# Attention into GEGLU on one core: a new step order in the first two batches, and out-projections rotating over three PSUM banks

## The chip, the cores and the metric

The kernel runs on one core of a Trainium2 chip. The metric is the device time of one execution in microseconds. Times inside an execution come from one profiled run, counted from the start of its span.

## The reference

A causal attention with 16 extra "beacon" keys that every query may see, for 8 batches of 8 heads with 576 tokens of 64 channels, is followed by a GEGLU block on the 4608 tokens of 512 channels.

```python
k_all, v_all = [beacon_k, k], [beacon_v, v]              # 16 + 576 keys
scores = q @ k_all.T / sqrt(64)                          # causal mask on the 576
a = softmax(scores)
x = (a @ v_all) -> (4608, 512)                           # heads side by side
out = (gelu(x @ w_gate) * (x @ w_val)) @ w_out           # d_ff = 1536, float32 out
```

## The kernel before

**Data flow.** Per batch, the heads are taken in four pairs (`m` = 0 to 3). For a pair, `scores` computes the transposed scores in four chunks S0 to S3 (512, 480, 464 and 208 columns for each of the two heads) into one of two PSUM buffers of two banks (tag `s`), and ScalarE takes the exponential of each chunk straight out of it (L205). `mask` zeroes the diagonal blocks, on POOL (`a` steps, L293) or by a table on VectorE (`d` steps, L290). `sums` (Z) multiplies the exponentials by ones into the two `z` banks, and adds the values of the first 64 queries, for which it needs value tile 0 alone. `values` (V) multiplies by all five value tiles into the one `x` bank, in the tile order 0, 2, 4, 1, 3. `invert` (I: transpose, reciprocal, transpose back) and `scale` (M: one product for the z part, one for the x part) run on VectorE and write `xT_sb`. A batch's attention is written by hand as five strings of steps, one for each pair and a last one; each engine executes its own instructions in that order.

**Gate and value.** The tokens are then taken in nine chunks of 512. For each of 12 tiles `gate_val` does 4 + 4 matmuls into an `s` buffer, ScalarE applies gelu (`ge_sb`), VectorE multiplies (`hT_sb`, L386). `gate_val_first` does the first tile's three earlier k-steps, then a filler, and then the step that needs the last pair of heads.

**Out-projection.** `o(n)` issues the next `n` of 48 matmuls per chunk: four groups (`ti`) of 12 (`fi`), each group into `o_ps`, a bank of a pool with one buffer (tag `o`). After a group VectorE copies it out (L424) and SyncE's queue writes it to `out` (L426). `O12` and the like are such calls within attention. At the end, `o(4)` follows each gate tile of the last chunk, and `o(OUT_UNITS)` does the last chunk's own 48.

**Loads.** POOL issues the loads, in order and interleaved with its masks: `r` a pair's q and k of batch 0, `y` a value tile of batch 0 (y0 also its beacon), `w` a third of the gate and value weights, `N3` three of the queued loads for the next batch. In batches 0 and 1, q and k are transposed on TensorE (`q1x`: pair 1's q through bank x; also o and z) and copied to `qkT` by VectorE (L246). `h3x` is three idle matmuls into bank x, `heat(n)` the same into bank o.

**What sets the order.** The step strings, the order of calls and the rotating PSUM and SBUF buffers: an instruction whose buffer is still being read waits, and with it all that is behind it on its engine.

Of the kernel before, what the change touches and what calls it, by code (L numbers as in the profile page):

```python
# [7 lines left out]
P = 128  # L8
B, H, S, NB, D = 8, 8, 576, 16, 64
SK = S + NB  # L10
N_TOK = B * S
D_MODEL = 512
D_FF = 1536
F_TILES = D_FF // P
K_CHUNKS = D_MODEL // P
CH = 512
N_CHUNKS = N_TOK // CH
NPAIR = H // 2
OUT_UNITS = (CH // P) * F_TILES
# [26 lines left out]
Z0 = 448  # L46
# [3 lines left out]
FP32 = mybir.dt.float32  # L50
# [8 lines left out]
def kernel(  # L59
# [12 lines left out]
    nc = tc.nc  # L72
    keep = tc.keep_in_program_order
# [7 lines left out]
    opool = ctx.enter_context(tc.tile_pool(name="opool", bufs=4))  # L81
    psum_s = ctx.enter_context(tc.tile_pool(name="psum_s", bufs=2, space=bass.MemoryType.PSUM))
    psum_x = ctx.enter_context(tc.tile_pool(name="psum_x", bufs=1, space=bass.MemoryType.PSUM))
    psum_o = ctx.enter_context(tc.tile_pool(name="psum_o", bufs=1, space=bass.MemoryType.PSUM))
# [11 lines left out]
    wo_sb = const.tile([P, F_TILES, D_MODEL], BF16, name="wo_sb", tag="wo_sb")  # L96
# [26 lines left out]
    def load_runs(b, m):  # L123
        for out_ap, in_ap in runs(b, m):
            dma(out_ap, in_ap)
# [75 lines left out]
    def mm(out_ap, lhsT, rhs, start, stop, **kw):  # L201
        keep(nc.tensor.matmul(out_ap, lhsT, rhs, start=start, stop=stop, **kw))  # L202
# [4 lines left out]
    def bank(tag, dtype, n, name):  # L207

        pool = psum_o if tag == "o" else psum_x
        if tag == "z":  # L210
            n *= 2
        return pool.tile([P, n], dtype, name=name, tag=tag)
# [108 lines left out]
    def sums(b, m):  # L321
        z_ps = z_of[b * NPAIR + m] = psum_x.tile([P, 1024], FP32, name="z_ps", tag="z")
        attend(b, m, z_ps, Z0, True, 0, SPLIT)
        attend(b, m, z_ps, Z0 + SPLIT, True, SPLIT, S)
        attend(b, m, z_ps, 0, False, 0, SPLIT, start=False)

    def values(b, m):
        x_ps = x_of[b * NPAIR + m] = psum_x.tile([P, S - SPLIT], FP32, name="x_ps", tag="x")
        attend(b, m, x_ps, 0, False, SPLIT, S)
# [32 lines left out]
    h_of, gv_of = {}, {}  # L362

    def gate_val_mms(ci, fi, kks):
        if fi == 0 and ci not in h_of:
            h_of[ci] = hpool.tile([P, F_TILES, CH], BF16, name="hT_sb", tag="hT_sb")
        if (ci, fi) not in gv_of:
            gv_of[ci, fi] = psum_s.tile([P, 2, CH], FP32, name="gv_ps", tag="s")
        gv_ps = gv_of[ci, fi]
        for w in range(2):  # L370
            for kk in kks:
                mm(
                    gv_ps[:, w, :],
                    (wg_sb, wv_sb)[w][:, kk, fi * P : (fi + 1) * P],
                    xT_sb[:, kk, ci * CH : (ci + 1) * CH],
                    kk == 0,
                    kk == K_CHUNKS - 1,
                    skip_group_check=True,
                )

    def gate_val_end(ci, fi):
        gv_ps = gv_of.pop((ci, fi))
        ge_sb = fpool.tile([P, CH], BF16, name="ge_sb", tag="ge_sb")
        act(ge_sb, gv_ps[:, 0, :], ACT.Gelu)
        keep(
            nc.vector.tensor_tensor(  # L386
                out=h_of[ci][:, fi, :], in0=gv_ps[:, 1, :], in1=ge_sb, op=ALU.mult
            )
        )

    def gate_val(ci, f0, f1):
        for fi in range(f0, f1):
            gate_val_mms(ci, fi, range(K_CHUNKS))
            gate_val_end(ci, fi)

    def gate_val_first(ci, fill, n, tiles=1):

        for fi in range(tiles):
            gate_val_mms(ci, fi, range(K_CHUNKS - 1))
        fill(n)  # L400
        for fi in range(tiles):
            gate_val_mms(ci, fi, [K_CHUNKS - 1])
            gate_val_end(ci, fi)

    out_done = [0]
    o_ps_of = [None]

    def o(n):
        for _ in range(n):
            ci, u = divmod(out_done[0], OUT_UNITS)  # L410
            ti, fi = divmod(u, F_TILES)
            if fi == 0:
                o_ps_of[0] = psum_o.tile([P, D_MODEL], FP32, name="o_ps", tag="o")
            o_ps = o_ps_of[0]
            mm(
                o_ps,
                h_of[ci][:, fi, ti * P : (ti + 1) * P],
                wo_sb[:, fi, :],
                fi == 0,
                fi == F_TILES - 1,  # L420
            )
            if fi == F_TILES - 1:
                o_sb = opool.tile([P, D_MODEL], FP32, name="o_sb", tag="o_sb")
                keep(nc.vector.tensor_copy(o_sb, o_ps))  # L424
                n0 = ci * CH + ti * P
                keep(nc.sync.dma_start(out=out[n0 : n0 + P, :], in_=o_sb))  # L426
            out_done[0] += 1

    def exp_table():
        keep(nc.scalar.preload_act_table_set(SET_EXP))  # L430
# [4 lines left out]
    def attention(b, *slots, extra=None):  # L435


        for m, slot in enumerate(slots):
            for step in slot.split():
                kind, n = step[0], step[1:]  # L440
                if kind == "S":
                    scores(b, m, *(int(c) for c in n))
                elif kind == "Z":
                    sums(b, int(n or m - 1))
                    if not n:
                        invert(b, m - 1)
                elif kind == "I":
                    invert(b, int(n))
                elif kind == "V":
                    values(b, int(n or m - 1))  # L450
                    if not n:
                        scale(b, m - 1)
                elif kind == "M":
                    scale(b, int(n))
                elif kind == "O":
                    o(int(n))
                elif kind in "adkq":
                    extra[kind](b, *n)
                else:
                    extra[kind](*n) if kind in "kqrwLhyad" else extra[kind](n)  # L460
# [9 lines left out]
            out=ident,  # L470
            in_=ident,
# [10 lines left out]
            out=tri,  # L482
            in_=tri,
# [4 lines left out]
            channel_multiplier=-1,  # L488
        )
    )  # L490
    for w, copies, n in ((0, [(S, dve_copy)], 0), (1, [(114, act_copy), (S, act_copy)], 1)):
        t0 = psum_s.tile([P, 2048], BF16, name="t0_ps", tag="s")
        trans(0, 0, w, t0, copies)
        heat(n)
# [3 lines left out]
    def load_next(n):  # L498
# [4 lines left out]
    extra = {  # L503
        "k": lambda b, m, tag: trans_in(tag, b, int(m), 1),
        "q": lambda b, m, tag: trans_in(tag, b, int(m), 0),
        "a": lambda b, m, c: mask(b, int(m), int(c)),
        "d": lambda b, m, c: mask(b, int(m), int(c), by_table=True),
        "r": lambda m: load_runs(0, int(m)),
        "h": lambda n, tag: heat(int(n), tag),
        "y": lambda t: load_v_tile(0, int(t)),  # L510
        "N": lambda n: load_next(int(n)),
# [3 lines left out]
    for m in range(1, NPAIR):  # L515
        queue.extend(runs(1, m))
    attention(
        0,
        "r2 h3x S0 k1o q1x S1 r3 y2 S2 d00 y0 q2o y1 k2x S3 d02 y3 d01 d03", "S0 y4 S1 w0 Z0 d10 S2 I0 a11 S3 k3x", "a12 S0 q3o S1 S2 a13 V0 M0 Z1 V1 w1 S3", "a21 I1 a20 a23 M1 S0 S1 a22 w2 Z2 V2 I2 S2 S3", "h3o a30 a31 a32 M2 a33 Z3 V3 I3 M3",
        extra=extra,  # L520
    )
    load_next(99)
    gelu_table()
    gate_val_first(0, heat, 2, 1)
    gate_val(0, 1, 7)
    trans_in("z", 1, 0, 1)
    gate_val(0, 7, 7 + 1)
    trans_in("x", 1, 0, 0)
    gate_val(0, 7 + 1, F_TILES)
    load_v(1)  # L530
    load_out_w()

    for b in range(1, B):
        exp_table()
        if b + 1 < B:
            queue.extend(qk_loads(b + 1))
        if b == 1:
            attention(b, "S0 S1 k1x a01 q1z S2 k3o d00 S3 d03 d02", "S0 N3 k2o S1 a11 a10 Z0 q2o I0 S2 a12 V0 M0 S3 a13", "S0 S1 q3o a21 Z1 I1 a20 S2 V1 a22 S3 M1", "S0 a23 S1 a30 a31 Z2 S2 I2 V2 a32 M2 S3 a33 O12", "Z3 N3 V3 I3 M3 N3 O12", extra=extra)
        elif b == 2:
            attention(b, "S0 O12 N3 S1 S2 O12 S3 N3", "S0 Z0 I0 S1 S2 O12 S3 V0 N3", "S0 S1 M0 Z1 V1 I1 S2 S3 O7", "S0 S1 M1 Z2 V2 I2 S2 S3 N2 M2", "O2 O3 Z3 I3 V3 M3 O12", extra=extra)  # L540
        else:
            attention(b, "O5 S0 S1 O7 S2 S3 O2 N3", "S0 S1 Z0 I0 V0 S2 M0 S3 O10 N3", "S0 S1 Z1 V1 I1 S2 S3 M1 O12 N3", "S0 S1 Z2 V2 I2 M2 S2 S3 O5 N2", "Z3 I3 V3 M3", extra=extra)
        gelu_table()
        if b + 1 < B:
            load_next(99)
            load_v(b + 1)
        gate_val_first(b, o, 0 if b == 1 else 0 if b == 2 else 7)
        if b + 1 < B:
            xbar_transpose(b + 1)
        gate_val(b, 1, F_TILES)  # L550
    o((N_CHUNKS - 2) * OUT_UNITS - out_done[0])
    for fi in range(F_TILES):
        gate_val(N_CHUNKS - 1, fi, fi + 1)
        o(4)
    o(OUT_UNITS)


# [28 lines left out]
```

## Time and profile before

| what | value |
|---|---|
| time, median of 3 runs | 408.98 us (407.93 to 410.36) |
| the profiled execution's own time | 410.23 us |
| its span, first to last instruction | 408.5 us |
| TensorE busy | 389.9 us, 95% of the span |
| ScalarE, VectorE, POOL busy | 189.2, 197.8, 163.9 us |
| mean granted TensorE clock | 0.982 |
| first gate and value matmul of batch 0, of batch 1 | 29.18 us, 76.53 us |
| start of the last four out-projection groups | 391.47, 395.01, 398.54, 402.07 us |

A row of the profile's groups gives the line, the engine and operation, the tiles written and read, the count, the busy time and the mean duration of one. Matmuls are pipelined: the 512-column ones take 379 ns each but follow each other every 216 ns, so that distances between starts say more than durations. A window's row gives the busy time of each engine (TensorE, its weight loads, VectorE, ScalarE, POOL, each with its number of instructions), then the granted TensorE clock, the DMA share and GB/s. A wait's row gives who waited for what: us in total, times, the longest.

### The profile page before, as it was taken

How to read it: one execution, taken by the hardware profiler on the slowest of the kernel's cores; microseconds unless marked ns; L12 is line 12 of the kernel's file. 1: busy time of each engine (PE TensorE's matmuls, PEld its weight loads, DVE VectorE, ACT ScalarE, POOL GpSimd, SP SyncE). 2: the span in 40 equal slices, each digit the busy share in tenths (PEclk: the TensorE clock that was granted, in tenths of full speed). 3: DMA queues.
4: the chain of work that ended last, by engine and by line, in shares of the span. 5: the costliest groups of instructions: out<-in, count | busy, mean ns of one | idle time of the engine just before them, and what ended most of it. 6: DMA issues, size and time to landing. Idle time of an engine off the chain costs nothing.

```text
span 408.5 us, 6704 instructions
## 1 busy us (share of the span) xinstructions
PE 389.9 (95%) x2665; PEld 179.2 (44%) x2665; DVE 197.8 (48%) x341; ACT 189.2 (46%) x255; POOL 163.9 (40%) x296
## 2 busy tenths in 40 slices
PE   7789979999999999999999999999999999999975
PEld 3444444444444444444444444444444444444432
DVE  2674458543473446543654266435733564333321
ACT  3743368135653387238633764366534853312200
POOL 8767134901871069404960297019900420000000
PEclk9799979999999999999999999999999999999999
DMA  7999950990989249962997099909991100001012
GB/s 98 180 181 173 153 62 4 155 160 9 147 77 162 38 48 133 111 109 37 128 123 114 27 100 129 137 8 112 105 148 36 54 27 26 0 27 51 26 53 77
DMA packets 139279, 36.19 MB, mean 89 GB/s; under 512 B 126960, under 2 KB 134640, under 8 KB 139248
## 3 DMA queue, kind: packets, MB, share of 16 engines
q0 software_dynamic: 104112, 19.15, 59.4%
q1 hardware_dynamic: 35136, 16.62, 18.3%
q8 instruction: 21, 0.34, 0.4%
q14 instruction: 10, 0.08, 0.1%
HBM read 38.27 MB, written 9.44 MB: 117 GB/s over the span
## 4 chain that ended last, share of the span: by engine, by line
PE 89%; DVE 4%; ACT 2%; POOL 2%; DMA 1%; issue 1%; POOLq 0%; DVEq 0%
PE gv_ps L202 46%; PE o_ps L202 24%; PE s_ps L202 7%; PE z_ps L202 6%; PE x_ps L202 5%; DVE o_sb L424 2%; DMA v_sb<-in_v_dram 1%; ACT expT L205 1%; DVE zt L337 1%; DVE rec L342 1%; PE t_ps L223 1%; POOL q L114 1%; POOL k L114 1%; DVE xT_sb L354 0%; POOL v_sb L114 0%
## 5 line engine op out<-in xcount | busy, mean ns | idle before, releaser
L205 ACT ACTIVATE ge_sb<-gv_ps 128x512 bf16<-128x512 f32 x108 | 64.5, 598 | 158.9 <-PE gv_ps L202 158.9
L386 DVE TENSOR_TENSOR hT_sb<-gv_ps,ge_sb 128x512 bf16<-128x512 f32 x108 | 74.7, 692 | 118.0 <-ACT ge_sb L205 118.0
L293 POOL TENSOR_SCALAR_AFFINE_SELECT expT<-expT 128x256 bf16<-128x256 bf16 (+2 forms) x151 | 55.4, 395 | 163.8 <-ACT expT L205 149.6
L205 ACT ACTIVATE expT<-s_ps 128x1024 bf16<-128x1024 f32 (+3 forms) x128 | 103.3, 862 | 36.4 <-PE s_ps L202 33.7
L202 PE MATMUL gv_ps<-xT_sb,wg_sb 128*128 128x512 bf16 x432 | 112.2, 379 | 0.3 <-DVE xT_sb L354 0.3
L202 PE MATMUL gv_ps<-xT_sb,wv_sb 128*128 128x512 bf16 x432 | 112.2, 379 | 0.0
L202 PE MATMUL o_ps<-wo_sb,hT_sb 128*128 128x512 bf16 x432 | 103.3, 380 | 4.0 <-DVE o_sb L424 3.8
L202 PEld LDWEIGHTS <-wv_sb 128*128 128x128 bf16 x432 | 42.3, 98 | 51.5 <-issue 0.6
L202 PEld LDWEIGHTS <-wg_sb 128*128 128x128 bf16 x432 | 41.6, 98 | 50.8 <-issue 1.6
L202 PEld LDWEIGHTS <-hT_sb 128*128 128x128 bf16 x432 | 40.0, 98 | 52.3 <-issue 6.9
L424 DVE COPY o_sb<-o_ps 128x512 f32<-128x512 f32 x36 | 24.9, 690 | 44.5 <-PE o_ps L202 44.5
L202 PE MATMUL s_ps<-qkT 64*128 64x80 bf16 (+5 forms) x384 | 41.9, 292 | 4.7 <-ACT expT L205 3.2
L337 DVE STREAM_TRANSPOSE zt<-z_ps 128x576 f32<-128x576 f32 x32 | 25.1, 783 | 28.6 <-PE z_ps L202 28.6
L114 POOL DMA_DIRECT2D v_sb<-in_v_dram x40 | 34.0, 889 | 0.0
L202 PE MATMUL z_ps<-expT,ones 80*64 80x80 bf16 (+5 forms) x384 | 30.5, 295 | 1.0 <-DVE xT_sb L354 0.9
L202 PEld LDWEIGHTS <-qkT 64*128 64x128 bf16 x384 | 14.8, 95 | 36.5 <-issue 32.9
L202 PE MATMUL x_ps<-expT,v_sb 128*64 128x512 bf16 (+4 forms) x320 | 28.8, 311 | 0.0
L114 POOL DMA_DIRECT2D k_sb<-in_k_dram x30 | 25.7, 855 | 0.8 <-DMA out_dram<-o_sb 0.3
L114 POOL DMA_DIRECT2D q_sb<-in_q_dram x30 | 25.8, 860 | 0.2
L342 DVE STREAM_TRANSPOSE rec<-rz 128x576 f32<-128x576 f32 x32 | 24.9, 778 | 1.1
L354 DVE TENSOR_TENSOR xT_sb<-x_ps,rec 128x512 bf16<-128x512 f32 x32 | 21.8, 681 | 1.8 <-PE x_ps L202 1.8
L202 PEld LDWEIGHTS <-ones 128*64 128x64 bf16 (+1 forms) x384 | 15.8, 113 | 13.5 <-issue 7.7
(36 smaller groups left out, 125.0 us busy)
## 6 DMA issues: line engine op xcount, KB each, us to landing
out_dram<-o_sb SPq DMA_DIRECT2D x36, 256.0 KB, 2.3
v_sb<-in_v_dram POOLq DMA_DIRECT2D x24, 128.0 KB, 5.2
q_sb<-in_q_dram POOLq DMA_DIRECT2D x24, 128.0 KB, 4.4
k_sb<-in_k_dram POOLq DMA_DIRECT2D x18, 128.0 KB, 4.8
wg_sb<-in_moe_w_gate_dram POOLq DMA_DIRECT2D x3, 512.0 KB, 7.0
wv_sb<-in_moe_w_val_dram POOLq DMA_DIRECT2D x3, 512.0 KB, 8.6
wo_sb<-in_moe_w_out_dram POOLq DMA_DIRECT2D x1, 1536.0 KB, 14.0
q<-in_q_dram POOLq DMA_DIRECT2D x8, 144.0 KB, 5.4
```

The lines of the kernel that those rows point to most:

```text
L114: keep(nc.gpsimd.dma_start(out=out_ap, in_=in_ap))
L202: keep(nc.tensor.matmul(out_ap, lhsT, rhs, start=start, stop=stop, **kw))
L205: keep(nc.scalar.activation(out_ap, in_ap, func, **kw))
L223: keep(nc.tensor.transpose(out_ap, in_ap, ident[0:n, 0:n]))
L293: nc.gpsimd.affine_select(out=d, in_=d, pattern=[[0, 2], [1, DIAG[t]]], compare_op=ALU.is_ge, fill=0.0, base=base, channel_multiplier=-1,)
L337: keep(nc.vector.transpose(zt, z_of[i][:, Z0 : Z0 + S]))
L342: nc.vector.transpose(rec.rearrange("p (n j) -> p n j", j=32), rz.unsqueeze(2).to_broadcast([P, NBLK, 32]))
L354: nc.vector.tensor_tensor(out=xT_sb[:, m, b * S + q0 : b * S + q1], in0=acc[:, 0 : q1 - q0], in1=rec[:, q0:q1], op=ALU.mult,)
L386: nc.vector.tensor_tensor(out=h_of[ci][:, fi, :], in0=gv_ps[:, 1, :], in1=ge_sb, op=ALU.mult)
L424: keep(nc.vector.tensor_copy(o_sb, o_ps))
```

## The change

In batch 0's strings, value tile y0 is loaded ahead of pair 3's q and k, y4 and y1 to y3 follow in another order, pair 0's S1 and S2 come ahead of two transposes, S3 behind those of pair 2, and the sums of pair 0 come after pair 1's S1. One heating matmul is added ahead of k's first transposes and one behind them; three in the last string and two in the first gate tile are left out. Batch 1's strings are reordered in the same manner (a transposition of q earlier, three loads earlier, one heating matmul), batch 2's slightly. The transpositions for batch 1 stand two and three gate tiles later.

The out-projections outside of attention, from the last chunk but one on, take their bank by `tags[ti % 3]` from o, x and z. Three in place of four out-projection matmuls follow each gate tile of the last chunk. The very last group is done by `o_last` in two halves of 256 columns, in banks o and x, each with a copy and a write of its own (the first from ScalarE's queue).

```diff
-    def o(n):
+    def o(n, tags="o"):
...
             if fi == 0:
-                o_ps_of[0] = psum_o.tile([P, D_MODEL], FP32, name="o_ps", tag="o")
-            o_ps = o_ps_of[0]
+                o_ps_of[0] = bank(tags[ti % len(tags)], FP32, D_MODEL, "o_ps")
+            o_ps = o_ps_of[0][:, 0:D_MODEL]
...
+    def o_last():
+
+        ci, ti = N_CHUNKS - 1, CH // P - 1
+        n0 = ci * CH + ti * P
+        half = D_MODEL // 2
+        for x, tag in enumerate("ox"):
+            cols = slice(x * half, (x + 1) * half)
+            o_ps = bank(tag, FP32, CH, "o_ps")[:, 0:half]
+            for fi in range(F_TILES):
+                mm(o_ps, h_of[ci][:, fi, ti * P : (ti + 1) * P], wo_sb[:, fi, cols], fi == 0, fi == F_TILES - 1)
+            o_sb = opool.tile([P, half], FP32, name="o_half", tag="o_half")
+            keep(nc.vector.tensor_copy(o_sb, o_ps))
+            keep((nc.scalar, nc.sync)[x].dma_start(out=out[n0 : n0 + P, cols], in_=o_sb))
...
-    for w, copies, n in ((0, [(S, dve_copy)], 0), (1, [(114, act_copy), (S, act_copy)], 1)):
+    for w, copies, n in ((0, [(S, dve_copy)], 1), (1, [(114, act_copy), (S, act_copy)], 2)):
...
-        "r2 h3x S0 k1o q1x S1 r3 y2 S2 d00 y0 q2o y1 k2x S3 d02 y3 d01 d03", "S0 y4 S1 w0 Z0 d10 S2 I0 a11 S3 k3x", "a12 S0 q3o S1 S2 a13 V0 M0 Z1 V1 w1 S3", "a21 I1 a20 a23 M1 S0 S1 a22 w2 Z2 V2 I2 S2 S3", "h3o a30 a31 a32 M2 a33 Z3 V3 I3 M3",
+        "h3z r2 S0 S1 k1o q1z S2 k2x q2o y0 r3 y4 y1 S3 d01 a00 y2 a02", "S0 a03 S1 Z0 y3 d10 I0 w0 S2 k3x a11 S3", "S0 a13 a12 q3o S1 S2 V0 M0 w1 Z1 V1 I1 M1 S3 a20", "S0 S1 a21 a22 a23 Z2 V2 I2 M2 w2 S2 S3 a31", "a30 a32 a33 Z3 I3 V3 M3",
...
-    gate_val_first(0, heat, 2, 1)
-    gate_val(0, 1, 7)
+    gate_val_first(0, heat, 0, 1)
+    gate_val(0, 1, 10)
     trans_in("z", 1, 0, 1)
-    gate_val(0, 7, 7 + 1)
+    gate_val(0, 10, 10 + 1)
     trans_in("x", 1, 0, 0)
-    gate_val(0, 7 + 1, F_TILES)
+    gate_val(0, 10 + 1, F_TILES)
...
-            attention(b, "S0 S1 k1x a01 q1z S2 k3o d00 S3 d03 d02", "S0 N3 k2o S1 a11 a10 Z0 q2o I0 S2 a12 V0 M0 S3 a13", "S0 S1 q3o a21 Z1 I1 a20 S2 V1 a22 S3 M1", "S0 a23 S1 a30 a31 Z2 S2 I2 V2 a32 M2 S3 a33 O12", "Z3 N3 V3 I3 M3 N3 O12", extra=extra)
+            attention(b, "S0 N3 k1z S1 a01 q1x k3o d00 S2 a02 S3 q2o d03", "N3 S0 S1 k2o Z0 a11 S2 a10 I0 a12 V0 S3 M0", "S0 a13 q3o S1 a21 Z1 S2 h1o a20 I1 S3 a22 V1", "M1 S0 S1 a23 Z2 I2 a31 a30 V2 M2 S2 a32 S3 a33 O12", "Z3 I3 V3 M3 O12 N3", extra=extra)
         elif b == 2:
-            attention(b, "S0 O12 N3 S1 S2 O12 S3 N3", "S0 Z0 I0 S1 S2 O12 S3 V0 N3", "S0 S1 M0 Z1 V1 I1 S2 S3 O7", "S0 S1 M1 Z2 V2 I2 S2 S3 N2 M2", "O2 O3 Z3 I3 V3 M3 O12", extra=extra)
+            attention(b, "S0 O12 N3 S1 S2 O12 S3 N3", "S0 Z0 S1 S2 I0 O12 S3 N3 V0", "S0 S1 M0 Z1 V1 S2 S3 O6 I1", "S0 M1 S1 Z2 V2 I2 S2 M2 S3", "O2 O4 Z3 V3 I3 N2 M3 O12", extra=extra)
...
-    o((N_CHUNKS - 2) * OUT_UNITS - out_done[0])
+    o((N_CHUNKS - 2) * OUT_UNITS - out_done[0], "oxz")
     for fi in range(F_TILES):
         gate_val(N_CHUNKS - 1, fi, fi + 1)
-        o(4)
-    o(OUT_UNITS)
+        o(3, "oxz")
+    o(OUT_UNITS, "oxz")
+    o_last()
```

## The prediction

> **What bounds the kernel now.** I read the engine table first, then the clock row, the chain of waits, the waits table, and the timeline and windows of the two stretches where TensorE is idle.
>
> ```profile
> PE 389.9 (95%) x2665; PEld 179.2 (44%) x2665; DVE 197.8 (48%) x341; ACT 189.2 (46%) x255; POOL 163.9 (40%) x296
> PEclk9799979999999999999999999999999999999999
> PE 89%; DVE 4%; ACT 2%; POOL 2%; DMA 1%; issue 1%; POOLq 0%; DVEq 0%
> ```
>
> TensorE is the bound: 389.9 of 408.5 us, and 89% of the chain. Only two things can be won: its 18.6 us of idle time, and time in which it is busy at a low clock (the two 7s in the clock row). By the windows view the idle time is 7.0 us before 35, 2.8 us between 50 and 70, 7.2 us after 380, and 1.6 us elsewhere.
>
> ```profile
> PE o_ps L202 <- DVE o_sb L424: 3.8, 5, 1.1
> PE s_ps L202 <- ACT expT L205: 3.2, 11, 0.5
> PE z_ps L202 <- DMA v_sb<-in_v_dram: 1.6, 1, 1.6
> ```
>
> ```profile
> 391.47 2.75 PE L202 MATMUL o_ps<-wo_sb,hT_sb 128*128 128x512 bf16 x12 [1.15 <-DVE o_sb L424]
> 394.26 0.69 DVE L424 COPY o_sb<-o_ps 128x512 f32<-128x512 f32 x1 [2.84 <-PE o_ps L202]
> 395.01 2.75 PE L202 MATMUL o_ps<-wo_sb,hT_sb 128*128 128x512 bf16 x12 [0.78 <-DVE o_sb L424]
> 404.86 0.69 DVE L424 COPY o_sb<-o_ps 128x512 f32<-128x512 f32 x1 [2.84 <-PE o_ps L202]
> ```
>
> The tail: each out-projection group of 12 matmuls waits until VectorE has copied the one bank out, four times running.
>
> ```profile
> 11.62:15.03 3.41, 1.55 (x22) 0.81 (x18) 1.82 (x7) 2.29 (x3) 3.08 (x6) 1.00 2.30 154
> 15.03:18.45 3.42, 3.19 (x39) 1.82 (x40) 2.78 (x6) 2.21 (x3) 1.49 (x3) 0.51 1.42 200
> 18.45:21.86 3.41, 3.41 (x28) 1.83 (x26) 1.35 (x3) 1.97 (x3) 1.78 (x5) 0.50 1.24 206
> 52.58:55.99 3.41, 2.03 (x48) 1.50 (x48) 2.19 (x5) 3.38 (x5) 0.00 (x0) 1.00 0.17 27
> 55.99:59.41 3.42, 2.90 (x31) 1.43 (x32) 2.33 (x7) 2.90 (x4) 2.95 (x5) 0.51 0.19 14
> 59.41:62.82 3.41, 3.41 (x38) 1.81 (x35) 1.99 (x4) 1.20 (x2) 1.42 (x4) 0.50 1.08 70
> ```
>
> The start: second column TensorE's busy time, third from the end its clock. Twice, a thin stretch (1.55 and 2.03 us busy of 3.41) is followed by 6.8 us at half clock, in batch 0's attention and in batch 1's. The windows before and after with 2.35 us busy or more were not followed by one.
>
> [...]
>
> **Part 1, the tail.** Before, the last gate group issues 389.30 minus its 1.73 us; four o matmuls follow and would end issuing at 390.17. The next group starts at 391.47, so 1.30 us are lost; the other three start 3.53 us apart for 12 x 0.216 = 2.59 us of issue, 0.94 lost each. Sum 1.30 + 3 x 0.94 = 4.1 us. After: the loop puts 3 in place of 4 matmuls behind each gate step, so its end comes 12 x 0.216 = 2.59 us earlier, and 12 matmuls of chunk 7's fourth group are left to cover the last gelu (0.60) and product (0.69). Groups take o, x, z by ti % 3, and ti is 3 then 0 at the chunk's border: both take bank o, so one wait of 0.94 stays. The groups of ti 0, 1, 2 and the halves (o, x) each find a bank freed two groups before. So 4.1 - 0.9 = 3.2 us gained. The last group in halves: [...]nothing, if the weight loads (98 ns) stay hidden; unhidden, [...]+2.4 us[...]. I take +0.05. The copy that ends the chain goes from 512 to 256 columns: the 64- and 512-column products take 0.224 and 0.681, so 1.02 ns a column, and the copy falls from 0.69 to about 0.42: -0.27. The last write moved its 256 KB in about 0.7 of its 2.0 us; half of that is about -0.3; the first half leaves earlier on ScalarE's idle queue. **Tail: -3.7 us** (-1.3 to -4.0).
>
> **Part 2, batch 0.** All q, k, v and weight transfers are issued by POOL in order. Moving y0 (two transfers) ahead of r3 (two), y1 and y2: before, q3, k3, v2, the beacon and v0 landed between 11.1 (k2, read off the k transpose at 11.09) and 15.1, 544 KB in 4.0 us. v0 is now ahead of q3, k3 and v2 (416 KB), so it lands 3.1 us earlier, near 12.0; the wait of 1.58 us goes. Next late: k2. S3 of pair 0 is now behind the transposes of k2 and q2, so it cannot start before 11.09 + 0.49 + 0.38 = 12.0, and ScalarE, which is then done with S0 to S2 (exps 1.02, 0.97, 0.94 from 8.0), idles from 10.9 to 12.2. From there I walk the queues with the rows' durations (S0 to S3 0.3, 0.3, 0.3, 0.2 on TensorE; transposes 0.5 and 0.4; Z and V 0.8 each; exps as above, S3 0.51):
>
> exps of pair 0's S3 at 12.2, pair 1's four 12.8 to 16.2, pair 2's S0 16.2 to 17.2. Z0 at 13.2 (its mask a03 is done by POOL at 13.2). Pair 2's S2 takes the score buffer that S0 leaves at 17.2, V0 runs 17.6 to 18.4, Z1 from 18.4. Before, Z1 began at 20.7 and the first gate's last matmuls at 31.41. The chain between them, Z, invert (0.8 + 0.3 + 0.8 on VectorE), scale's first part 0.23, then Z again, three times, is the same in both orders: 3.2 us a turn, 10 us with everything at full clock (before, Z1 itself ran at half). So the gate's last step comes at 28.4 with no low clock: -3.0 us.
>
> With the low clock: the new order has 1.8 us of work between 8.2 and 11.6 (q1, k1, S2, then nothing until k2 lands at 11.09), thinner than what tripped before. On the same grid the spell runs 11.6 to 18.4. In it q2, S3, S0, S1, Z0, S2, k3 take double: pair 1's S0 is computed 13.3, its S2 (behind Z0, 15.4) 16.0, pair 2's S0 17.7, exp to 18.9, V0 19.3, Z1 20.1, gate 30.1: **-1.3 us**. I take this one.
>
> Costs hidden: y3 waits on POOL behind a03 and is issued at 13.2 to 14.0; with 4.3 to 6.2 us to landing it is there at 17.5 to 19.5, while V0's last two matmuls want it at 18.2 (full clock, up to 1.3 us lost) or 20.0 (low clock, nothing). w0 is issued about 1.5 us later, lands near 23 to 24, wanted at 26: covered by 2 us; w1 and w2 have more. The extra heat ahead of k's transposes fits in the wait for k (5.24 to 5.95); that behind them puts S0 0.1 us later (counted: exps from 8.0, not 7.84). The five removed heats lay ahead of waits (0.51 and 0.33 us on VectorE), the one added in batch 1 costs 0.22 at most (in the 0.7 above). Moving the z transposes from after tile 6 to after tile 9 leaves the q copy 2.2 us after its transposes begin, before ScalarE's exp table is in: nothing.
>
> **Part 3, batch 1.** ScalarE has its table at 54.0 and four pairs of exps, 3.4 us each. With the gate's end kept at 52.0 for comparison, the new order (S1 after one transpose, q2 before pair 1's scores, I1 after S2) walks to the next gate's first matmul at 73.8 at full clock; before it was 76.5. On the same grid, shifted by 1.3 us, the window 53.9 to 57.3 holds 2.0 us of work and trips again; k2, Z0, S2, V0, S3, S0 then run at half speed to 64.1, and the walk ends at 76.6. **0 us**, with -2.7 as the other end and +0.7 above (the spell lies in denser work). The N3 in slot 0 has POOL's idle time before 56 (14 us idle); the N3 that stays ahead of a11 holds POOL to 60.1, and Z1 wants a11's mask at 61.4 or later. Those transfers go to a ring slot that nobody reads yet.
>
> **Part 4, batch 2.** The 60 o matmuls are cut otherwise (7, 2, 3 become 6, 2, 4), I0, V0 and I1 are shifted; TensorE has 0.4 us idle there, of which 0.27 lies in slot 0, untouched. 0, within 0.3 either way (I1 may make Z2 late).
>
> **Sum:** -3.7 - 1.3 + 0 + 0 = -5.0 us. The profiled execution took 410.23 us (span 408.5 and 1.7 around it), the upper end of the runs (407.93 to 410.36); it becomes 405.2, and the median 404.0. Two spells' shifting place would explain such a spread.
>
> **Rivals.**
> A, forecast, 0.64: both spells stay, 404.0, 402.6 to 405.4 with the spread of runs.
> B, 0.22: the extra heats and the denser order lift one or both spells. -3.7 - 3.0 - 2.7 = -9.4 with both, so 399.6; with one about 402. For it: the windows at 2.35 us stayed up, a small margin. Against: both thin stretches come from waits (k2's landing, the table load) that no edit takes away.
> C, 0.11: the tail does less than it says, the half-width weight loads lie bare (+2.4), or one more spell falls in the first gate, whose two heats were removed: 6.8 us at half clock, all on the path, +3.4. 406.4 to 407.4.
> D, 0.03, slower: low clock at the gates. Each spell there costs 3.4 us in full; two more than today give -5.0 + 6.8 = +1.8 (410.8), still no difference, three +5.2 (414.2). It decides from the third. Against it: once a gate runs, it is busy 3.41 of 3.41 us.
> That the banks do not rotate (pools serialising them) would leave -1.9, 407: in C.
>
> A difference of 0.5% (2.0 us) is about what a measurement here can tell. Faster by more, 0.90 (A, B, part of C); within, 0.07; slower, 0.03. Range 400.4 to 406.5: A with its spread, most of B, the near end of C. I put the time at 403.8, A with a little of its lower side.
>
> **What would show it.** Right: o_ps waits on o_sb down from five to two, one of 0.8 us near 390; the last copy about 0.42 us; no z_ps wait for v_sb; the gate's first step near 30; low clock from about 11.6 or a window beside it, and again in batch 1. Wrong: 256-column matmuls over 0.15 us apart, an x_ps wait for v_sb over 1 us, or low clock after 30 in a gate.

## The result, and the profile after

The changed kernel takes 402.46 us (median of 4 runs, 401.96 to 403.17) where the kernel before takes 409.14 (407.93 to 410.36): a ratio of 0.9838, 95% interval 0.9804 to 0.9872. That is 6.7 us or 1.6% less. The forecast was 403.8 in a range of 400.4 to 406.5. The profiled execution took 403.17 us, with a span of 401.5.

The same parts of the page of the changed kernel: engines, clock, chain.

```profile
PE 387.7 (97%) x2675; PEld 179.8 (45%) x2675; DVE 197.1 (49%) x338; ACT 188.9 (47%) x255; POOL 164.9 (41%) x300
PEclk9899969999999999999999999999999999999999
PE 91%; DVE 4%; DMA 1%; POOL 1%; ACT 1%; issue 1%; POOLq 0%
```

TensorE is still the bound. Its busy time fell by 2.2 us although 10 matmuls were added: the stretches at a clock of 0.50 within it are 10.2 us long in all, for 13.7 before. Its idle time fell from 18.6 to 13.8 us.

Four rows of its waits (who waited for what: total, times, longest):

```profile
PE z_ps L202 <- DVE xT_sb L354: 1.3, 1, 1.3
PE o_ps L202 <- DVE o_sb L425: 1.1, 2, 0.8
PE t_ps L223 <- DMA k<-in_k_dram: 0.9, 1, 0.9
PE gv_ps L202 <- DVE xT_sb L354: 0.8, 1, 0.8
```

The wait of z_ps for v_sb is gone, and k2's landing is the wait in its place, as forecast. The o_ps waits went from five to two. The 1.3 and 0.8 us are the z bank and the last pair, late at the end of batch 0 now that TensorE has less to do there.

The timeline of the end:

```profile
387.35 10.55 PE L202 MATMUL o_ps<-wo_sb,hT_sb 128*128 128x512 bf16 x60 [0.78 <-DVE o_sb L425]
396.63 0.42 DVE L441 COPY o_half<-o_ps 128x256 f32<-128x256 f32 x1 [0.62 <-PE o_ps L202]
397.09 0.37 ACTq L442 DMA_DIRECT2D out_dram<-o_half  x1
397.94 0.42 DVE L441 COPY o_half<-o_ps 128x256 f32<-128x256 f32 x1 [0.89 <-PE o_ps L202]
398.39 0.33 SPq L442 DMA_DIRECT2D out_dram<-o_half  x1
```

One wait of 0.78 us, bank o taken twice running; then 60 matmuls without a gap.

The windows around the two thin stretches (second column TensorE's busy time, third from the end its clock):

```profile
8.96:12.37 3.41, 1.97 (x49) 1.28 (x44) 2.51 (x6) 2.76 (x5) 3.41 (x6) 1.00 1.63 172
12.37:15.78 3.41, 3.41 (x37) 1.92 (x37) 2.23 (x7) 2.43 (x3) 3.41 (x7) 0.50 2.05 135
15.78:19.20 3.42, 2.91 (x44) 1.69 (x46) 2.61 (x6) 3.42 (x5) 2.64 (x7) 1.00 1.16 179
49.95:53.36 3.41, 1.96 (x46) 1.33 (x45) 3.10 (x7) 3.38 (x5) 0.00 (x0) 0.99 1.60 170
53.36:56.80 3.44, 3.44 (x45) 2.22 (x46) 1.70 (x5) 3.01 (x4) 3.27 (x6) 0.50 0.46 29
56.80:60.20 3.40, 3.40 (x28) 1.17 (x26) 2.69 (x6) 1.44 (x3) 1.85 (x5) 0.51 1.65 108
```

Again each low spell follows a window of which under 60% was busy (1.97 and 1.96 us of 3.41), and the two starts, 12.37 and 53.36, lie 41.0 us apart, 12 times 3.41, as 15.03 and 55.99 do in the profile before. In batch 0 the spell is one window long here (3.41 us), not two (6.83). Being thin is not enough to tell, though: the window from 22.60 us on, 2.14 us busy, was followed by no spell in this profile (the clock is 1.00 from 15.78 to 53.33).

The two timelines laid side by side, by starts of TensorE's matmuls:

| mark | before | after | gained up to it |
|---|---|---|---|
| last k-step of batch 0's first gate tile | 31.41 | 28.82 | 2.59 |
| first gate matmul of batch 1 | 76.53 | 72.77 | 3.76 |
| out-projection group ahead of the last chunk's gate | 356.50 | 352.74 | 3.76 |
| end of the span | 408.5 | 401.5 | 7.0 |

So the profile puts 2.6 us in batch 0, 1.2 in batch 1, nothing in batches 2 to 7 and 3.2 in the tail. What it can't say is how much of the first two is the order and how much the clock.

### The profile page after: what moved, and what is told of

Its sections match the earlier page's. It is cut to its first block, busy times and chain, and to the rows that moved or that the text cites. A ratio compares the mean times of both kernels' runs of the same rounds, so it can differ in the third digit from the quotient of the medians.

```text
span 401.5 us, 6727 instructions
## 1 busy us (share of the span) xinstructions
PE 387.7 (97%) x2675; PEld 179.8 (45%) x2675; DVE 197.1 (49%) x338; ACT 188.9 (47%) x255; POOL 164.9 (41%) x300
## 4 chain that ended last, share of the span: by engine, by line
PE 91%; DVE 4%; DMA 1%; POOL 1%; ACT 1%; issue 1%; POOLq 0%
PE gv_ps L202 46%; PE o_ps L202 24%; PE z_ps L202 7%; PE s_ps L202 7%; PE x_ps L202 5%; DMA k<-in_k_dram 1%; DVE o_sb L425 1%; PE t_ps L223 1%; ACT expT L205 1%; DVE zt L337 1%; DVE rec L342 1%; POOL q L114 0%; DVE xT_sb L354 0%; DVE qkT L246 0%; DVE rz L339 0%
## 5 line engine op out<-in xcount | busy, mean ns | idle before, releaser
L293 POOL TENSOR_SCALAR_AFFINE_SELECT expT<-expT 128x256 bf16<-128x256 bf16 (+2 forms) x155 | 57.0, 398 | 157.6 <-ACT expT L205 145.1
L202 PE MATMUL o_ps<-wo_sb,hT_sb 128*128 128x512 bf16 (+1 forms) x444 | 102.8, 374 | 1.3 <-DVE o_sb L425 1.1
L202 PEld LDWEIGHTS <-hT_sb 128*128 128x128 bf16 x444 | 41.2, 98 | 48.2 <-issue 3.4
L354 DVE TENSOR_TENSOR xT_sb<-x_ps,rec 128x512 bf16<-128x512 f32 x32 | 21.8, 681 | 1.0 <-PE x_ps L202 1.0
```

Of the source, the lines that this page charges most:

```text
L293: nc.gpsimd.affine_select(out=d, in_=d, pattern=[[0, 2], [1, DIAG[t]]], compare_op=ALU.is_ge, fill=0.0, base=base, channel_multiplier=-1,)
L354: nc.vector.tensor_tensor(out=xT_sb[:, m, b * S + q0 : b * S + q1], in0=acc[:, 0 : q1 - q0], in1=rec[:, q0:q1], op=ALU.mult,)
```

## The experiments

Beside its time every run has its mean granted clock. A spell is a stretch at a clock of 0.50, one or two windows of 3.41 us long in the profiles before and after, so 2 x (1 - clock) x time is the time that a run is recorded at half clock, called low time below; a mean clock of 0.996 comes to one such window, 0.978 to five. Over the 72 runs of the kernel before that were measured beside these experiments the low time was 11.7 us on average, the time 408.76 us (406.18 to 410.48), and a straight line through them rises by 0.22 us for each us of low time. "At equal clock" means read from such lines, where they meet zero low time; that point is uncertain by 0.2 to 0.4 us (standard error) for the kernels with 12 runs or more. Each figure for other kernels rests on 4 to 20 runs.

Low time leaves out the start. In the profiles before and after the first eight heating matmuls, from 1.26 us on, take 634 ns each and follow each other every 0.42 us, twice the 0.216 of later ones, while the clock column says 1.00. In twelve of the 14 profiles the heating matmuls ahead of the first S0, at 6.3 to 6.9 us, run at the later rate (four in 1.04 us, five in 1.25 to 1.29). In the other two (the old order, heated, and the tail alone) four take 1.89 us, and twelve transposes 0.68 and 0.69 us as late as 9.88 and 9.43, for 0.45 from 11.10 and 10.86 on; this is called a late start below. A mean clock of 1.000, which the first of the two has, therefore says that there was no spell, not that the start was early. Low time also counts low clock behind the last matmul, where it costs TensorE nothing: 0.9 us in the profile before, from 407.56 on.

### The tail alone

The kernel before with the edits of `o`, `o_last` and the last calls only:

```diff
-                o_ps_of[0] = psum_o.tile([P, D_MODEL], FP32, name="o_ps", tag="o")
+                o_ps_of[0] = bank(tags[ti % len(tags)], FP32, D_MODEL, "o_ps")
...
-        o(4)
-    o(OUT_UNITS)
+        o(3, "oxz")
+    o(OUT_UNITS, "oxz")
+    o_last()
```

> The kernel before with only the out-projection edits of the end (three banks, three per gate tile, the last group in halves). Theory (the gains of the parts add up, and each is a wait that is gone): -3.2 us, as between the two profiles (412.0 to 408.5 in span terms: the last chunk's stage 3.2 us shorter, everything up to the last chunk as before). Rival (the end gains only because the core comes to it earlier or warmer): under 2 us. The low clock of the start stays as in the kernel before, mean granted clock 0.982 or so.

The figures 412.0 and 408.5 in it are a slip; the two profiles have 52.0 and 48.8 us from the third mark of the table to the end. Measured: ratio 0.9934 (0.9907 to 0.9961); mean 405.43 us with 11.4 to 17.9 us of low time in 8 of 12 runs. Its line meets zero low time at 402.9, that of the kernel before (49 runs on that chip) at 406.0: **-3.1 us** at equal clock. In its profile the third mark is at 355.49 and the span's end at 404.2: 48.7 us, as in the changed kernel. The tail is worth 3.1 to 3.3 us, the same with the old and the new order ahead of it.

### Batch 0 alone, batch 1 alone

The kernel before with batch 0's five new strings (the first is shown), the heats ahead of them and the first gate without its two:

```diff
-        "r2 h3x S0 k1o q1x S1 r3 y2 S2 d00 y0 q2o y1 k2x S3 d02 y3 d01 d03"
+        "h3z r2 S0 S1 k1o q1z S2 k2x q2o y0 r3 y4 y1 S3 d01 a00 y2 a02"
...
-    gate_val_first(0, heat, 2, 1)
+    gate_val_first(0, heat, 0, 1)
```

> The kernel before with only batch 0's new strings and its heating matmuls. Theory (waits for v0 and for ScalarE gone): the first gate's last step comes at 28.8 where it came at 31.4, and the time falls by 2.6 us. Rival (clock): the part of the gain that the prediction did not have, 1.3 us, comes from one low-clock window in place of two; then runs differ by about 1 us with their mean granted clock, and the gain at equal clock is 1.3 to 1.6 us.

Measured: ratio 0.9959 (0.994 to 0.9978), mean 406.97 us of 20 runs with 8.6 us of low time. At equal clock -1.0 us (405.0 for 406.0), the rest of the 1.8 us in the mean from less low time (8.6 us for 12.0 in the 49 runs on that chip). Neither side of the expectation has its number: the clock's share is there, but the order is worth less than the 1.3 us that I had.

And with batch 1's new strings (the first is shown) and the later transpositions for it, each three gate tiles later:

```diff
-    gate_val(0, 1, 7)
+    gate_val(0, 1, 10)
...
-"S0 S1 k1x a01 q1z S2 k3o d00 S3 d03 d02"
+"S0 N3 k1z S1 a01 q1x k3o d00 S2 a02 S3 q2o d03"
```

> The kernel before with only batch 1's new string and the later transpositions for it in the first gate. Theory: the order itself gives 1.2 us (second gate's first matmul at 75.4 where it came at 76.5). Rival, as predicted: nothing, since the low clock stays for two windows; the 1.2 us of the profiles is then where the low-clock windows fall, and moves between -0.7 and +2.7 from run to run.

Measured: ratio 0.996 (0.9938 to 0.9981), mean 407.18 us of 20 runs; at equal clock -1.2 us. The order itself gains, as the first theory had it, and the forecast's zero falls.

The three parts at equal clock: 3.1 + 1.0 + 1.2 = 5.3 us. The 8 runs of the changed kernel (the four of the result and those of the next section) have 8.9 us of low time where the kernel before has 11.7: 2.8 x 0.22 = 0.6 us more. Together 5.9; the means, 408.76 and 402.62, differ by 6.1. The agreement is looser than it looks. The changed kernel's own line is steeper (0.30) and meets zero low time at 400.0, which is 6.2 below the 406.2 of the kernel before, so that at zero the parts fall 0.9 us short of the whole; their errors together are of that size, and what else could make it up is not shown.

### The changed kernel again, and the extra heats

> The changed kernel once more, so that the next three have it on the same chip, and for more of its runs with their clocks. If the parts add up (tail alone -3.1 us at equal clock, batch 0 alone -1.0, batch 1 alone -1.2, from the straight lines of time over low-clock time), it is 5.3 us faster at equal clock, and its mean 402 to 403 us; the runs should lie on a line of 0.24 us for each us at half clock.

Measured: 404.12 and 404.23 us with 13.7 us of low time, 401.26 and 401.28 with 4.0. One program, 3 us apart, by its spells; the steps are about 0.3 us per us. With the four earlier runs the line meets zero at 400.0. The mean came as expected; the 5.3 us at equal clock came out as 6.2, and the 0.24 us per us as 0.30.

```diff
-    for w, copies, n in ((0, [(S, dve_copy)], 1), (1, [(114, act_copy), (S, act_copy)], 2)):
+    for w, copies, n in ((0, [(S, dve_copy)], 0), (1, [(114, act_copy), (S, act_copy)], 1)):
```

> The changed kernel without the two heating matmuls added around the first transposes of k (one and two back to none and one). Theory (they keep the clock up at the start): a lower mean clock and up to 0.8 us more. Rival, as predicted: S0 starts 0.1 us earlier and nothing else changes.

Measured: 401.81 us on average, 3.2 to 13.7 us of low time, 400.3 at zero. No more spells than with the heats and no difference at equal clock: the two heating matmuls that the change added ahead do nothing that four runs can show.

### Heating the thin stretches

The first strings of batch 0 and of batch 1 in the changed kernel:

```diff
-"h3z r2 S0 S1 k1o q1z S2 k2x q2o y0 r3 y4 y1 S3 d01 a00 y2 a02"
+"h3z r2 S0 S1 k1o q1z S2 h4x k2x q2o y0 r3 y4 y1 S3 d01 a00 y2 a02"
...
-"S0 N3 k1z S1 a01 q1x k3o d00 S2 a02 S3 q2o d03"
+"S0 N3 k1z h2x S1 a01 q1x k3o d00 S2 a02 h2z S3 q2o d03"
```

> The changed kernel with eight idle heating matmuls in its thin stretches: four ahead of the transposes of k2 in batch 0, two ahead of S1 and two ahead of S3 in batch 1. Theory[...]: the mean granted clock rises from 0.989 to 0.995 or more, and the time falls by (8.9 - 4) x 0.24 = 1.2 us. Rival (low clock follows from something else than the busy share, or the heats stand in the way of real work): clock as before, time the same or up by 0.2 to 0.9 us.

Measured: 400.11 us (399.94 to 400.33), ratio to the kernel before 0.9798 (0.976 to 0.9836), mean clock 0.998 to 1.000 in all runs. The changed kernel lost 2.5 us of its mean, twice the 1.2 expected, since the spells went entirely. Windows of the same stretches in its profile:

```profile
8.20:11.61 3.41, 3.08 (x62) 1.88 (x61) 1.88 (x5) 2.58 (x3) 3.41 (x6) 1.00 1.38 151
11.61:15.02 3.41, 2.66 (x42) 1.34 (x37) 2.98 (x8) 3.29 (x5) 3.41 (x7) 1.00 1.93 140
48.60:52.01 3.41, 2.98 (x52) 1.76 (x50) 2.81 (x6) 3.38 (x4) 0.00 (x0) 1.00 1.29 181
52.01:55.42 3.41, 3.19 (x55) 1.77 (x53) 2.21 (x7) 3.28 (x5) 2.95 (x6) 1.00 1.23 94
```

The formerly thin stretches (first and third row) are 90% and 87% busy and the clock stays up. Eight idle matmuls, placed where TensorE waits anyway, take the spells away and with them the 3 us of scatter. In all 22 runs of the five heated kernels, this one and those below, the mean clock is 0.998 or more, where the unheated ones have 0.978 to 0.996. Heats in the thin stretches are all that the heated kernel adds to the changed one, so here the thin stretches caused the spells; the two don't only go together.

### The old order, heated

The second string of batch 0 and the first of batch 1 in the kernel before:

```diff
-"S0 y4 S1 w0 Z0 d10 S2 I0 a11 S3 k3x"
+"S0 y4 S1 w0 h5x Z0 d10 S2 I0 a11 S3 k3x"
...
-"S0 S1 k1x a01 q1z S2 k3o d00 S3 d03 d02"
+"S0 h4o S1 k1x a01 q1z h2o S2 k3o d00 S3 h2x d03 d02"
```

> The kernel before, its order untouched, with 13 idle heating matmuls in its thin stretches: five ahead of Z0 in batch 0, four ahead of S1, two ahead of S2 and two behind S3 in batch 1. Theory (the two new orders win 2.2 us at equal clock, and about 1 us more on average through fewer low-clock windows): 406.0 us at full clock, 5.9 above the heated changed kernel. Rival (the orders win only through the clock, the gate's last step comes at 28.0 with either order once no window is low): about 403.2, only the tail's 3.2 above the heated changed kernel.

Measured: 406.27 us (406.00 to 406.42), clock 1.000 in all four runs: 6.2 us above the heated changed kernel, for 5.9 expected. At the same time heats alone, with nothing reordered, give the kernel before a ratio of 0.9927 (0.9901 to 0.9953).

How much of the 6.2 us is batch 0's order can't be read from this, for two reasons that the profile shows. TensorE was slow until about 10 us, as said above. Four heats there, and the same four in a profile of the old strings of batch 0 with an early start (batch 1 alone):

```profile
6.91 1.89 PE L202 MATMUL heat<-warm 128*128 128x512 bf16 x4
```

```profile
6.69 1.04 PE L202 MATMUL heat<-warm 128*128 128x512 bf16 x4
```

And the five heats ahead of Z0 stand in the way of work: Z0's value matmuls run at 15.42 with no wait for v_sb, where in the tail's profile, also with a late start but without heats, they run at 14.53, after such a wait. The gate's last k-step came at 29.69. Without heats, spell and late start (batch 1 alone) the old strings reach it at 27.98, and the new ones without a spell in five profiles at 27.76 to 28.16. So for batch 0 the rival stands as far as these profiles go; for batch 1 it falls.

Batch 1 can be compared spell for spell, from its first S0 to the next gate's first matmul:

| low windows in batch 1's attention | old order | new order |
|---|---|---|
| none (old: two heated profiles; new: three heated and one not) | 22.40 us | 21.18 us |
| one (batch 0 alone; batch 1 alone) | 23.50 us | 22.39 us |
| two (two profiles; four profiles) | 24.53, 24.55 us | 23.22 to 23.36 us |

The new order gains 1.1 to 1.3 us in each row, and a low window costs 0.8 to 1.2 us in either order. In the new order heats cost nothing here; whether they do in the old is not shown, but the rows with spells have none. ScalarE's timeline shows half of the gain. First the old order, then the new, both heated (start, us, exponentials merged, idle before):

```profile
52.30 5.15 ACT L205 ACTIVATE expT<-s_ps 128x1024 bf16<-128x1024 f32 x6
57.76 3.37 ACT L205 ACTIVATE expT<-s_ps 128x928 bf16<-128x928 f32 x4 [0.32 <-PE s_ps L202]
61.61 1.52 ACT L205 ACTIVATE expT<-s_ps 128x928 bf16<-128x928 f32 x2 [0.47 <-PE s_ps L202]
63.47 3.13 ACT L205 ACTIVATE expT<-s_ps 128x1024 bf16<-128x1024 f32 x4 [0.34 <-PE s_ps L202]
```

```profile
50.36 9.78 ACT L205 ACTIVATE expT<-s_ps 128x1024 bf16<-128x1024 f32 x12
60.48 1.89 ACT L205 ACTIVATE expT<-s_ps 128x1024 bf16<-128x1024 f32 x2 [0.34 <-POOL expT L293]
62.70 1.35 ACT L205 ACTIVATE expT<-s_ps 128x928 bf16<-128x928 f32 x2 [0.33 <-PE s_ps L202]
```

In the new order twelve exponentials run without a gap; the last ends 13.7 us after the first began, 14.3 in the old. The other 0.6 us lie between the last exponential and the gate (5.5 us for 6.1).

### Batch 0's order at full clock

The heated kernel before with batch 0's strings of the heated changed kernel (again the first of five; the `h5x` of the old second string goes, and the heats ahead of the strings and the first gate without its two come with it):

```diff
-"r2 h3x S0 k1o q1x S1 r3 y2 S2 d00 y0 q2o y1 k2x S3 d02 y3 d01 d03"
+"h3z r2 S0 S1 k1o q1z S2 h4x k2x q2o y0 r3 y4 y1 S3 d01 a00 y2 a02"
```

> The heated kernel before (batch 1 and the end in their old form, batch 1's heats kept) with batch 0 in the new order and its four heats in place of the old order and its five. At full clock in every run, so that batch 0's order is measured without the low clock. Theory A (the straight lines over low-clock time): 1.0 us faster than the heated kernel before, 405.2. Theory B (the two heated profiles, 29.69 to 27.76 at the first gate's last step): 1.9 us faster, 404.3. Rival (full clock alone does it, since one profile of the old order reached that step at 27.98 with no low window ahead of it): no difference, 406.2.

Measured: 406.09 to 406.29 us in three runs, 404.44 to 404.78 in the other three; mean 405.39, 0.9 below the heated kernel before. The mean agrees with theory A, but the runs lie in two groups 1.5 us apart, one at the rival's figure and one near B's, and the low time, 1.6 us in the upper group and 0 to 0.8 in the lower, is too little for it. A late start, which low time leaves out, is a candidate. The profiled run is of the lower group: its first twelve transposes, at 4.70, took 0.45 us, not 0.69, and it reached the gate's last step at 28.10. There is no profile of the upper group, so what sets the groups stays open. Theory B rested on the 29.69 of the heated old order, which has a late start and the heats' own time in it. So batch 0's order is worth about 1 us on average over the executions that occur; that it gains with full speed throughout is not shown.

### Value tile 0

```diff
-"h3z r2 S0 S1 k1o q1z S2 h4x k2x q2o y0 r3 y4 y1 S3 d01 a00 y2 a02"
+"h3z r2 S0 S1 k1o q1z S2 h4x k2x q2o r3 y0 y4 y1 S3 d01 a00 y2 a02"
```

> The heated changed kernel with value tile 0 loaded behind pair 3's q and k again (the one step r3 y0 in place of y0 r3). Theory (the transfers land in order): v0 lands 288 KB or about 2.1 us later, near 14.5, Z0's last two matmuls, which ran at 13.5, wait about 1 us for it, and the time is 0.7 to 1 us longer. Rival (v0 is not late, the slack of ScalarE takes it up): no difference.

Measured: 400.26 us (400.01 to 401.53). Three of the four runs are as in the heated changed kernel, the fourth is 1.3 us longer, which stays open. The profile, of a run of 400.05 us, has no wait for v_sb. Z0's value matmuls in its timeline:

```profile
13.57 0.22 PE L202 MATMUL z_ps<-expT,v_sb 128*64 128x64 bf16 x2
```

They start at 13.57 for 13.46 with y0 ahead, so v0, issued at 8.20, had landed by then. The landing near 14.5 that was expected falls: v0 may land later, but not late. In the new order Z0 stands behind pair 1's S1 and tile 2 is no longer ahead of tile 0; which of the two makes the place relative to r3 harmless in this run was not tested. In the old strings, too, the wait for v_sb differs between executions: 1.58 us in the profile before, 0.52 and 0.37 with batch 1 alone and the tail alone.

### The last group, and the bank that is taken twice

```diff
-    o(OUT_UNITS, "oxz")
-    o_last()
+    o(OUT_UNITS + F_TILES, "oxz")
```

> The changed kernel with its last group in one piece of 512 columns, in bank o. Theory of the prediction: the halves gain 0.27 in the copy and 0.3 in the write, so this is 0.6 us slower than the changed kernel. Rival, from the profile after (last copy's end to the span's end 3.1 us, 2.9 before): the write's fixed part is all that counts and the halves gain 0.1 to 0.3 us.

Measured: 402.79 us on average with 10.2 us of low time, 402.62 with 8.9 for the changed kernel: the same at equal clock, within 0.3 us. From the last copy's start to the span's end the profiles have 3.66 us with the whole group and 3.51 to 3.56 with halves. So the halves gain 0.1 us: the copy its 0.27, but the span ends 3.1 us after the last write's issue, where it ended 2.9 after the whole one's. The half itself landed 1.7 us after its issue and the whole one 2.0, so the 0.3 us of the prediction are there and are lost again behind the landing.

```diff
-                o_ps_of[0] = bank(tags[ti % len(tags)], FP32, D_MODEL, "o_ps")
+                o_ps_of[0] = bank(tags[(4 * ci + ti) % len(tags)], FP32, D_MODEL, "o_ps")
```

> The changed kernel with the bank taken by a running number of the group, (4 * ci + ti) % 3, so that the fourth group of a chunk and the first of the next take different banks. Theory (the wait of 0.78 us that is left, with 0.16 of the pipeline's end, is bank o taken twice running): 0.9 us faster, no o_ps wait for o_sb after 380. Rival (the copy and product of VectorE are late there anyway): no gain, another wait in its place.

Measured: 401.22 us on average with 8.0 us of low time, 1.4 below the changed kernel and 0.6 to 1.2 at equal clock. Its timeline has one row where there were two:

```profile
382.77 13.79 PE L202 MATMUL o_ps<-wo_sb,hT_sb 128*128 128x512 bf16 x75
```

75 matmuls from the last gate step to the end, and no gap. Without the clock's scatter it can be weighed better, with this edit in the heated changed kernel:

> The heated changed kernel with the banks by a running number of the group, to have a version that is better than both. Both theories: the two gains add, 400.1 - 0.9 = 399.2 us, mean granted clock 0.998 or more. If the heats only moved the low clock to other windows, the mean clock falls under 0.995 in some of the runs.

Measured: 399.11 us (398.98 to 399.40), 1.0 below the heated kernel, for 0.9 expected; mean clock 0.999 to 1.000. **This version beats both**: ratio to the kernel before 0.9755, interval 0.9733 to 0.9776.

## Why the prediction was right, and where it was off

**The bound and the direction** were right: the gains are TensorE's idle time and low clock, and the slower rivals (C, D) did not come: the half-width matmuls hid their loads (18 in 2.13 us, with 98 ns for a load), and the profile after has no spell in a gate (the clock is 1.00 from 15.78 to 53.33 and from 60.16 to the end). Rival B, fewer spells, came in part: in the profile after, batch 0's spell has one window for two. The extra heats have no part in it that four runs show, and a second profile of the same kernel has both windows, so this was luck.

**The tail, -3.7 forecast, -3.1 to -3.3 measured.** Three of the four waits went and one of 0.78 stayed at bank o, as derived from `ti % 3`; with the running number it goes too, which proves the derivation. The half-width matmuls did hide their weight loads of 98 ns (the second half's copy starts 1.31 us after the first's, 12 x 109 ns, and half of the full width's 216 is 108). Mis-sized was the last write: -0.3 from half the bytes, +0.2 measured at the span's end.

**Batch 0, -1.3 forecast, -2.6 in the profile, about -1.0 at equal clock.** The two walks were good. At full clock the gate's step was put at 28.4; the profiles of the new order without a spell have 27.76 to 28.16. With two low windows it was put at 30.1; the profiles with two have 29.56 and 29.77, those with one 28.43 to 28.82. Good, too, was the choice to have the spell in both orders: two windows against two is 31.41 to about 29.7, or -1.7. What was off is "the spell runs 11.6 to 18.4" as a fixed fact: place and length differ between executions (15.03 to 21.86 before, 13.2 to 20.0 in the changed kernel's second profile, 17.6 to 21.0 with the tail alone), the profile after had one window, 12.37 to 15.78, and that one window makes -2.6 of it. The full-clock walk was compared with the 31.41 of an old order that had a spell, so that its -3.0 holds the spell's cost as well; the old strings without one reach the step at 27.98 in the one profile that has neither heats nor a late start, which leaves no gain in that state. "The wait of 1.58 us goes" was right, but that wait is 0.37 to 0.52 in other executions of the old strings, and the place of y0 relative to r3 has no part in it that the profile shows.

**Batch 1, 0 forecast, -1.2 measured.** The full-clock walk was good: 21.8 us from S0 to the gate, 21.18 measured without a spell. The walk with the spell, 24.6, was not: measured 23.22 to 23.36. It made two low windows cost 2.8 us where they cost 2.1; a reason could be that the spell came 3.9 us behind S0, not 5.3, over less dense work, which was not tested. I compared that walk with a measured 24.5 and read "nothing"; a comparison of both orders without a spell, 22.40 and 21.18, would have shown the order's gain.

**Batch 2** 0, as forecast: between the second and the third mark of the table nothing is gained. So the sum, -5.0 forecast and -6.7 measured, missed batch 1's 1.2 us; about 0.6 us more goes with less low time.

That low time fell from 11.7 to 8.9 us is weakly shown with 8 runs against 72: on the chip of the second four the kernel before had 8.8 us itself.

## What to carry to other kernels

Read the mean granted clock of each run before comparing orders: one spell of two windows decides more (about 2 us in batch 1 here) than either reordering (1.0 and 1.2), and in batch 0 it began anywhere from 11.2 to 17.6 us in the profiles. Look at the distance of the first matmuls, too, since a late start doesn't show in the clock (1.000 in the old order, heated, with four heats in 1.89 us for 1.04). Where TensorE has thin stretches that no edit can fill with work, fill its waits with idle matmuls in a free bank (2.5 us of the mean here), and compare orders in that state, with an eye on heats that stand in the way of work. When banks rotate by an index within a chunk, check the step from the last index to the first (a wait of 0.78 us here).

## What the runs showed of the hardware that I had not expected

In the profiles before and after the clock went to 0.50 four times while TensorE had work, once for 3.4 us and three times for 6.8, and in the 3.41 us ahead TensorE was busy for 1.55, 2.03, 1.97 and 1.96 us, that is 45% to 60%. No busy share divides the cases: 2.07 us (the whole last group's profile, from 21.47) and 2.14 us (the profile after, from 22.60) brought no spell, while 2.35 us did (batch 0 alone, from 51.18; twelve sums take 1.55 us from 54.49 on, for 0.88 later). The case of 2.14 us holds no transposes on TensorE, that of batch 0 alone 1.1 us of them; but the window from 8.21 in the profile before, with 1.76 us of transposes among 2.35 busy, brought none either, so what sets a spell off stays open. Eight matmuls of 0.2 us each undid the spells (mean clock 0.998 to 1.000 for 0.983 to 0.995). The time lost is 0.22 (the kernel before) to 0.30 us (the changed kernel) for each us at half clock by the lines over the runs, less than half. And a write of half the size did not end the span earlier: the data of the 256 KB moved in 0.75 us and those of the 128 KB in 0.5, but from its issue to the span's end it took 0.2 us longer; why stays open.
